# Attention scores of even and odd heads: from one half of the array's rows after the other to both by turns

## The chip, the cores and the metric

The kernel runs on one core of one Trainium2 chip. The core has a matrix engine (TensorE, PE in the profile, with its weight loads listed apart as PEld), a vector engine (VectorE, DVE), a scalar engine (ScalarE, ACT), GpSimd (POOL) and a queue engine (SyncE, SP) that issues most transfers. Matrix products land in PSUM, which is split into banks. The metric is the device time of one execution in microseconds. Three timed runs of the kernel before gave 1156.94, 1159.72 and 1166.53 us, median 1159.72.

## The reference

A retention layer without softmax feeds two mixture-of-experts layers. The part that the change touches is the first:

```python
batch, n_heads, seq, head_dim = (8, 8, 576, 64)
scores = scale * np.matmul(q, k.transpose(0, 1, 3, 2))
Dmat = np.where(rel >= 0, gamma[:, None, None] ** rel[None, :, :], 0.0)
ret = scores * Dmat[None, :, :, :]
return np.matmul(ret, v).astype(np.float32)
```

Its result, 4608 tokens of 512 numbers, goes through two layers that each pick one of eight experts for a token by the largest of eight gate logits, and multiply by that expert's two matrices (512 x 1024 and 1024 x 512). Because the choice is an argmax, the attention is computed to nearly single precision: every factor is split into a high and a low half-precision part, and a product is three products (high by high, high by low, low by high).

## The kernel before, in words

**Tiling.** `attention_and_routing` cuts the sequence of each batch into four chunks of 128 positions and a tail of 64; the tails of two batches make one more chunk, so there are 36 chunks (nine for two batches). A chunk is handled with all eight heads. Within a chunk the scores of key by query are computed, masked and multiplied by the values; what lies before the chunk comes in through a running state of 64 x 64 numbers a head. After that each token's row is scaled, gate logits are formed, a route is computed for groups of four or five chunks, and POOL scatters the rows by expert to DRAM. `experts` follows as a loop of its own, and takes most of the time.

**One chunk, by names.** `k_hi`, `k_lo`, `q_hi`, `q_lo` split the inputs (ACT and DVE). `transposes` (L330, eight products into `pt`) turns the keys, and `kT_out` copies them to `kT`. There a pair of heads lies one below the other: the even head in partitions 0 to 63, the odd head in 64 to 127, and the queries `qT` lie in the same way. `scores` (L348) multiplies them. `HALF[r]` picks the partitions, so with r = 0 a product uses rows 0 to 63 of the array and with r = 1 rows 64 to 127. For each r there are four head pairs and three products a pair, 12 products of 64 rows by 128 columns with 128 columns moving, into the PSUM tile `pa[r]`. The tags `pa0` and `pa1` have one buffer each, so a chunk's scores can't start before those of the chunk before have been read.

The two kinds are read differently. For even heads `a_full` (step `am0`, DVE, L418) masks straight from PSUM into a 32-bit tile (`a` in the profile), and `av_full` (`av0`, L402, product `po<-vs,a`) multiplies it at full precision. For odd heads `a_hi` (`ah1`, ACT, `au`) and `a_lo` (`al1`, DVE, L280, `al`) split, `mask` (`mh1`, `ml1`, POOL) masks, and `av` (`av1`, `po<-vh,ah` and `po<-vh,al`) multiplies. `qS` (`qS0`, `qS1`, product `po<-Sh,qT`) adds the state's share, `kv` (L375, L377) makes the next state in `pS`, which `Sn` (L381) scales. `out` (L429) reads `po` into `xg` once for each chunk. `lg` (L460) forms the gate logits from a row that a DMA has transposed.

**Order.** Nothing is scheduled at run time. `PLAN` gives each step five numbers, one for each position c of a chunk in its batch (the fifth is the tail); step n of chunk i is sorted at i + PLAN[n][c], and each engine gets its instructions in that order and works them off one after the other. The rows that the change touches are

```python
    "S0": (-0.000, -0.451, -0.122, 0.179, 0.057),
    "am0": (0.222, 0.032, 0.531, 0.449, 0.187),
    "S1": (0.334, 0.281, 0.287, 0.260, 0.137),
```

`S0` and `S1` are the scores of even and of odd heads: two steps, with other work between them on PE for most chunks.

Of the kernel before, what the change touches and what calls it, by code (L numbers as in the profile page):

```python
# [13 lines left out]
F32 = mybir.dt.float32  # L14
# [5 lines left out]
B, H, S, HD = 8, 8, 576, 64  # L20
D, F, E = 512, 1024, 8
N = B * S
P = 128
# [11 lines left out]
PLAN = {  # L35
    "k_hi": (-2.028, -2.770, -3.081, -2.909, -2.763),
    "vs": (-1.992, -2.348, -3.188, -1.669, -1.282),
    "k_lo": (-1.751, -2.064, -2.527, -2.579, -2.639),
    "q_hi": (-1.097, -1.702, -1.683, -2.485, -2.161),
    "pt": (-1.401, -1.677, -1.460, -1.290, -1.005),  # L40
    "v_hi": (-0.811, -1.371, -1.336, -0.862, -0.420),
    "q_lo": (-0.551, -1.252, -1.482, -1.253, -0.584),
    "v_lo": (-0.297, -1.046, -0.245, -0.372, 0.196),
    "kT": (-1.159, -0.874, -0.403, -0.701, -0.998),
    "S0": (-0.000, -0.451, -0.122, 0.179, 0.057),
    "am0": (0.222, 0.032, 0.531, 0.449, 0.187),
    "S1": (0.334, 0.281, 0.287, 0.260, 0.137),
    "kv": (0.073, 0.524, 0.372, 0.505, 1.633),
    "Sn": (0.230, 0.575, 0.613, 0.695, 6.213),
    "ah1": (0.596, 0.631, 0.385, 0.518, 0.232),  # L50
# [61 lines left out]
def attention_and_routing(tc, st, I, K):  # L112

    nc = tc.nc
# [3 lines left out]
    ps = psum("ps", 1)  # L118
# [152 lines left out]
    HALF = (slice(0, 64), slice(64, 128))  # L271
# [14 lines left out]
    class Chunk:  # L286
# [54 lines left out]
        def q_lo(self):  # L341
            lo(self.qT[:, 1], self.qn, self.qT[:, 0], QS)

        def scores(self, r):
            self.pa[r] = ps.tile([P, 512], F32, tag=f"pa{r}", name=f"pa{self.tag}_{r}")
            for hp in range(4):
                for n, (x, y) in enumerate(PASSES):
                    nc.tensor.matmul(self.pa[r][:, hp * P:(hp + 1) * P], self.kT[HALF[r], 4 * x + hp, :], self.qT[HALF[r], y, hp, :], start=(n == 0), stop=(n == 2))  # L348

        def a_hi(self, r):  # L350
            self.au[r] = three.tile([P, 512], F16, bufs=3, tag="au", name=f"au{self.tag}_{r}")
# [113 lines left out]
    for i, x in enumerate(order):  # L465
# [6 lines left out]
        "vs": Chunk.v_scale, "k_hi": Chunk.k_hi, "k_lo": Chunk.k_lo, "q_hi": Chunk.q_hi, "q_lo": Chunk.q_lo, "v_hi": Chunk.v_hi, "v_lo": Chunk.v_lo,  # L472
        "pt": Chunk.transposes, "kT": Chunk.kT_out, "kv": whole(Chunk.kv), "Sn": whole(Chunk.state),
        "Sh": whole(Chunk.state_hi), "Sl": whole(Chunk.state_lo), "out": Chunk.out, "sq": Chunk.squares,
        "rs1": Chunk.row_scale, "rs2": Chunk.row_scale2, "xh": Chunk.x_hi, "xl": Chunk.x_lo, "lg": Chunk.logits,
    }
    for n, f, r in (("S0", Chunk.scores, 0), ("S1", Chunk.scores, 1), ("am0", Chunk.a_full, 0), ("av0", Chunk.av_full, 0),
                    ("qS0", Chunk.qS, 0), ("qS1", Chunk.qS, 1), ("ah1", Chunk.a_hi, 1), ("al1", Chunk.a_lo, 1), ("av1", Chunk.av, 1)):
        parts[n] = lambda x, f=f, r=r: f(x, r)
    for n, part in (("mh1", 0), ("ml1", 1)):  # L480
# [5 lines left out]
    for i, x in enumerate(order):  # L486
        for L in "kqv":
            add(i - 5.5, x.load, L)
        for n, beats in PLAN.items():
            when = beats[x.c]  # L490
            if i >= NT - 2:
                when = {"qS0": PLAN["S1"][x.c] - 0.001, "qS1": PLAN["av1"][x.c] + 0.001}.get(n, when)
            if n in ("k_hi", "k_lo", "q_hi", "q_lo", "vs", "v_hi", "v_lo") and i < len(FIRST):
                when += FIRST[i]
            add(i + when, parts[n], x)
# [923 lines left out]
def build(nc, I, off, outs):  # L1419
    with ExitStack() as st:  # L1420
        sb = lambda n, s, dt: st.enter_context(nc.sbuf_tensor(n, s, dt))[:]
        K = {"off": off}
        K["cst"] = sb("cst", [P, max(b for _, b in off.values())], F32)
        K["ones"], K["tri"] = sb("ones", [P, P], F16), sb("tri", [P, P], F16)
        K["wg2"] = sb("wg2", [P, 4, 24], BF16)
        K["bias"] = sb("bias", [P, 16], F32)
        K["reg1"] = sb("reg1", [1, 24], I32)
        K["zero"] = sb("zero", [P, XW], F32)
        K["wb0"] = sb("wb0", [P, 2, 8192], F16)
        K["xs1"] = nc.dram_tensor("xs1", [E * R, XW], F32, kind="Internal").ap()  # L1430
        K["xs2"] = nc.dram_tensor("xs2", [E * R, XW2], F32, kind="Internal").ap()
        with tile.TileContext(nc) as tc, ExitStack() as s2:
            attention_and_routing(tc, s2, I, K)
        experts(nc, st, I, K, outs[0])
# [46 lines left out]
```

## Time and profile before

| | us |
|---|---|
| median of three timed runs | 1159.72 |
| lowest and highest | 1156.94, 1166.53 |
| the profiled execution | 1168.55 |
| span of the profiled execution, first to last instruction | 1166.8 |
| score products (L348), 864 of them, busy time | 84.5 |

The span falls into the attention and routing (to about 305 us), a change-over, and the experts from 327.5 us on. The profile's line PEclk gives the clock that TensorE was granted, as a share of full speed: 0.50 is 1.2 GHz and 1.00 is 2.4 GHz, and the trace shows only these two. In the attention the clock goes back and forth between them; in the experts it stands at 1.00 nearly throughout. Busy time of PE counts a product from its start to its end, and products overlap, so for the cost of a block of products the start of the block and the start of the next one are read from the timeline.

### The profile page before, as it was taken

What the parts mean: (1) busy time and instruction counts of PE and PEld (TensorE: products, weight loads), DVE (VectorE), ACT (ScalarE), POOL (GpSimd) and SP (SyncE); (2) the same over time, 40 slices, a digit from 0 to 9 for tenths busy, and PEclk for the clock granted to TensorE, in tenths of its full rate; (3) what the DMA queues carried; (4) which work ended last, traced back from release to release, by engine and by line L of the source; (5) the groups of instructions that cost most, each with busy time, mean ns of one, the idle gap of its engine ahead of it and who ended that gap; (6) DMA issues with size and microseconds to landing.
All of it is one profiled execution on the core that took longest, in us unless ns stands there. A gap on an engine that the chain in (4) does not pass through costs nothing. (4 is left out here: it accounts for less than half of the span.)

```text
span 1166.8 us, 27289 instructions
## 1 busy us (share of the span) xinstructions
PE 1083.7 (93%) x10037; PEld 788.2 (68%) x10037; DVE 572.4 (49%) x1624; ACT 441.6 (38%) x833; POOL 334.0 (29%) x370
## 2 busy tenths in 40 slices
PE   8999889998179999999999989999999999999996
PEld 6888778887156676666666657676766666767664
DVE  6567988996645555555555564641421211111211
ACT  5556656663324343443434433431411111111111
POOL 6456866885511211112121231211001000001000
PEclk6556768685589999999999999999999999999999
DMA  8254756675466665657466646435421121121110
GB/s 286 56 146 91 215 169 166 184 209 154 119 218 184 144 148 143 167 121 188 93 201 156 147 126 156 125 75 170 90 56 55 45 64 38 46 56 54 45 37 30
DMA packets 213056, 145.07 MB, mean 124 GB/s; under 512 B 174089, under 2 KB 174253, under 8 KB 212912
## 3 DMA queue, kind: packets, MB, share of 16 engines
q1 hardware_dynamic: 203952, 114.63, 39.9%
q0 software_dynamic: 8960, 28.62, 6.9%
q8 instruction: 79, 1.29, 0.5%
q14 instruction: 65, 0.53, 0.2%
HBM read 70.75 MB, written 33.92 MB: 90 GB/s over the span
## 5 line engine op out<-in xcount | busy, mean ns | idle before, releaser
L1060 PE MATMUL ph<-xT,wb 128*128 128x256 f16 (+2 forms) x1344 | 339.1, 263 | 22.4 <-PEq L564 22.4
L1061 PE MATMUL ph<-xT,wb 128*128 128x256 f16 (+2 forms) x1344 | 339.2, 263 | 0.0
L1062 PE MATMUL ph<-xT,wb 128*128 128x256 f16 (+2 forms) x1344 | 339.1, 263 | 0.0
L1268 DVE SCALAR_TENSOR_TENSOR hT<-ph,hT 128x512 f16<-128x512 f32 (+2 forms) x168 | 106.5, 638 | 333.7 <-DVEq L564 332.0
L1068 PE MATMUL py<-wb,hT 128*128 128x512 f16 x608 | 230.3, 379 | 1.2 <-issue 1.1
L1070 PE MATMUL py<-wb,hT 128*128 128x512 f16 x608 | 230.4, 379 | 0.0
L1069 PE MATMUL py<-wb,hT 128*128 128x512 f16 x608 | 230.4, 379 | 0.0
L1159 ACT ACTIVATE hT<-ph 128x512 f16<-128x512 f32 (+2 forms) x168 | 92.9, 553 | 227.2 <-ACTq L564 227.1
L1060 PEld LDWEIGHTS ph<-xT,wb 128*128 128x128 f16 x1344 | 131.7, 98 | 40.3 <-issue 23.1
L1061 PEld LDWEIGHTS ph<-xT,wb 128*128 128x128 f16 x1344 | 131.7, 98 | 17.1
L1062 PEld LDWEIGHTS ph<-xT,wb 128*128 128x128 f16 x1344 | 131.8, 98 | 13.1
L1386 POOL DMA_INDIRECT out_dram<-yo,idxo x37 | 35.9, 971 | 333.1 <-POOLq L564 329.7
L1375 POOL TENSOR_SCALAR idx<-v_pos 128x1 int32<-128x1 f32 x39 | 15.4, 394 | 336.3 <-POOLq L564 336.3
L1070 PEld LDWEIGHTS py<-wb,hT 128*128 128x128 f16 x608 | 59.4, 98 | 71.8
L1068 PEld LDWEIGHTS py<-wb,hT 128*128 128x128 f16 x608 | 59.3, 98 | 66.7 <-issue 1.2
L1069 PEld LDWEIGHTS py<-wb,hT 128*128 128x128 f16 x608 | 59.3, 98 | 64.9
L348 PE MATMUL pa<-qT,kT 64*128 64x128 f16 x864 | 84.5, 272 | 7.7 <-DVE al L280 6.1
L1153 ACT ACTIVATE yo<-py,v_gcol 128x512 f32<-128x512 f32 x37 | 25.4, 687 | 168.2 <-ACTq L564 168.2
L576 DVE SCALAR_TENSOR_TENSOR wb<-stg,wb 128x2048 f16<-128x2048 f32 x36 | 82.4, 2290 | 11.0 <-DVEq L564 11.0
L348 PEld LDWEIGHTS <-kT 64*128 64x128 f16 x864 | 69.4, 122 | 13.9 <-DVE al L280 6.8
L1136 ACT ACTIVATE wb<-stg 128x2048 f16<-128x2048 f32 x36 | 68.5, 1901 | 0.0
L1147 ACT ACTIVATE sq<-py 128x512 bf16<-128x512 f32 x39 | 23.3, 597 | 111.6 <-ACTq L564 111.6
(175 smaller groups left out, 1479.9 us busy)
## 6 DMA issues: line engine op xcount, KB each, us to landing
stg<-in_moe_w_dram SPq DMA_DIRECT2D x36, 1024.0 KB, 5.1
kn<-in_k_dram SPq DMA_DIRECT2D x36, 256.0 KB, 6.4
qn<-in_q_dram SPq DMA_DIRECT2D x36, 256.0 KB, 4.5
vn<-in_v_dram SPq DMA_DIRECT2D x36, 256.0 KB, 3.4
w0s<-in_moe_w_dram SPq DMA_DIRECT2D x16, 256.0 KB, 4.7
xs<-zero SPq DMA_DIRECT2D x8, 262.0 KB, 2.7
xs<-zero SPq DMA_DIRECT2D x8, 258.0 KB, 2.9
xT<-xs SPq DMA_TRANSPOSE x42
```

The lines of the kernel that those rows point to most:

```text
L348: nc.tensor.matmul(self.pa[r][:, hp * P:(hp + 1) * P], self.kT[HALF[r], 4 * x + hp, :], self.qT[HALF[r], y, hp, :], start=(n == 0), stop=( ...
L576: r = fn(*a, **kw).then_inc(self.sem, 1)
L1060: pe.matmul(o, w1(P_, 0)[:, c, fs], xT[s][:, c, cs], start=(c == 0), stop=False)
L1061: pe.matmul(o, w1(P_, 0)[:, c, fs], xT[s][:, 4 + c, cs], start=False, stop=False)
L1062: m = pe.matmul(o, w1(P_, 1)[:, c, fs], xT[s][:, c, cs], start=False, stop=(c == 3))
L1068: pe.matmul(py[b], hT[:, 0, f, bs], w2(P_, 0)[:, f, :], start=(f == 0), stop=False)
L1069: pe.matmul(py[b], hT[:, 0, f, bs], w2(P_, 1)[:, f, :], start=False, stop=False)
L1070: m = pe.matmul(py[b], hT[:, 1, f, bs], w2(P_, 0)[:, f, :], start=False, stop=(f == 7))
L1136: ac.activation(wb[P_ % 2][:, 0, 2048 * c:2048 * c + 2048], stg[:, 2048 * c:2048 * c + 2048], AF.Copy, scale=WS).then_inc(T["cv_full"])
L1159: ac.activation(hT[:, 0, 2 * g:2 * g + 2, cs], ph[g][:, :, cs], AF.Relu).then_inc(T["hh_full"])
L1268: stt(hT[:, 1, 2 * g:2 * g + 2, cs], ph[g][:, :, cs], 0.0, hT[:, 0, 2 * g:2 * g + 2, cs], op0=ALU.max, op1=ALU.subtract).then_inc(T["h_full"])
L1386: po.indirect_dma_start(out=out, out_offset=bass.IndirectOffsetOnAxis(ap=idxo[b], axis=0), in_=yo[b], in_offset=None, bounds_check=N - 1, ...
```

## The change

The steps `S0` and `S1` become one step `S`, which issues the products of even and odd heads by turns: the first of r = 0, the first of r = 1, the second of r = 0, and so on. Each kind still goes to its own bank. The step stands nearly where `S1` stood, and `am0` is moved behind it.

```diff
-    "S0": (-0.000, -0.451, -0.122, 0.179, 0.057),
-    "am0": (0.222, 0.032, 0.531, 0.449, 0.187),
-    "S1": (0.334, 0.281, 0.287, 0.260, 0.137),
+    "S": (0.222, 0.181, 0.287, 0.260, 0.097),
+    "am0": (0.334, 0.282, 0.531, 0.449, 0.187),
...
-        def scores(self, r):
-            self.pa[r] = ps.tile([P, 512], F32, tag=f"pa{r}", name=f"pa{self.tag}_{r}")
+        def scores(self):
+
+            for r in range(2):
+                self.pa[r] = ps.tile([P, 512], F32, tag=f"pa{r}", name=f"pa{self.tag}_{r}")
             for hp in range(4):
                 for n, (x, y) in enumerate(PASSES):
-                    nc.tensor.matmul(self.pa[r][:, hp * P:(hp + 1) * P], self.kT[HALF[r], 4 * x + hp, :], self.qT[HALF[r], y, hp, :], start=(n == 0), stop=(n == 2))
+                    for r in range(2):
+                        nc.tensor.matmul(self.pa[r][:, hp * P:(hp + 1) * P], self.kT[HALF[r], 4 * x + hp, :], self.qT[HALF[r], y, hp, :], start=(n == 0), stop=(n == 2))
...
-                when = {"qS0": PLAN["S1"][x.c] - 0.001, "qS1": PLAN["av1"][x.c] + 0.001}.get(n, when)
+                when = {"qS0": PLAN["S"][x.c] - 0.001, "qS1": PLAN["av1"][x.c] + 0.001}.get(n, when)
```

What that does to the order is seen on PE where chunk 0 of the second batch passes into chunk 1. A name such as `pa_0_1` is the score tile of position 0, odd heads; `kT_0` belongs to position 0. Before:

```order
L348 MATMUL pa_0_0_766<-qT_0_602,kT_0_600 128x128
...
L375 MATMUL pS_0_779<-vh_0_632,kh_0_465 64x64
...
L402 MATMUL po_3_713<-vs_3_388,a_3_674 128x64 x4
L348 LDWEIGHTS kT_0_600
L348 MATMUL pa_0_1_822<-qT_0_602,kT_0_600 128x128
...
L330 MATMUL pt_2_850<-id_69,kh_2_604 128x128
...
L348 MATMUL pa_1_0_859<-qT_1_660,kT_1_809 128x128
...
L402 MATMUL po_0_891<-vs_0_471,a_0_815 128x64 x4
...
L348 MATMUL pa_1_1_916<-qT_1_660,kT_1_809 128x128
```

And in the changed kernel, the same place:

```order
L377 MATMUL pS_0_766<-vh_0_632,kh_0_452 64x64
...
L404 MATMUL po_3_713<-vs_3_388,a_3_674 128x64 x4
L350 LDWEIGHTS kT_0_600
L350 MATMUL pa_0_0_802<-qT_0_602,kT_0_600 128x128
...
L350 MATMUL pa_0_1_803<-qT_0_602,kT_0_600 128x128
...
L329 MATMUL pt_2_850<-id_69,kh_2_604 128x128
...
L404 MATMUL po_0_878<-vs_0_458,a_0_833 128x64 x4
...
L350 MATMUL pa_1_0_895<-qT_1_660,kT_1_796 128x128
...
L350 MATMUL pa_1_1_896<-qT_1_660,kT_1_796 128x128
```

The even heads' scores of position 0 have moved behind the state products `pS_0` and the values' products `po_3`, those of position 1 behind the products `po_0`, and each block now holds both kinds. Between the block of position 0 and the products `po_0` that need its even half there remain the eight transposes and twelve products of `av`.

DVE at the same place (`al` reads odd scores, `a` even ones, `xg` reads a finished chunk). Before:

```order
L280 TENSOR_TENSOR al_0_1_889<-pa_0_1_822,au_0_1_873 128x512
L418 TENSOR_TENSOR a_1_908<-pa_1_0_859,mc 128x512
L429 TENSOR_TENSOR xg_3_910<-po_3_713,cst 128x512
L282 SCALAR_TENSOR_TENSOR kh_4_914<-kn_4_544,kh_4_914 128x512
L381 TENSOR_TENSOR Sn_1_969<-pS_1_942,cst 128x256
```

And in the changed kernel:

```order
L279 TENSOR_TENSOR al_0_1_876<-pa_0_1_803,au_0_1_860 128x512
L431 TENSOR_TENSOR xg_3_921<-po_3_713,cst 128x512
L420 TENSOR_TENSOR a_1_927<-pa_1_0_895,mc 128x512
L281 SCALAR_TENSOR_TENSOR kh_4_925<-kn_4_544,kh_4_925 128x512
L383 TENSOR_TENSOR Sn_1_969<-pS_1_942,cst 128x256
```

The masking `a_1` has moved behind `xg_3`. The orders of ACT and POOL are the same in both kernels.

## Rows read from the trace of the kernel before

**Rows 1.** The page: busy shares; the span in 40 slices of 29.2 us.
```profile
PE 1083.7 (93%) x10037; PEld 788.2 (68%) x10037; DVE 572.4 (49%) x1624; ACT 441.6 (38%) x833; POOL 334.0 (29%) x370
...
PEclk6556768685589999999999999999999999999999
```

**Rows 2.** Busy time by stretch, from:to, length, then engines, clock, DMA share, GB/s.
```profile
11.45:110.43 98.98, 98.98 (x1148) 86.63 (x1147) 61.65 (x130) 53.89 (x102) 54.19 (x59) 0.50 0.45 136
264.03:292.50 28.47, 26.39 (x331) 22.91 (x329) 17.81 (x57) 10.39 (x23) 13.36 (x15) 0.50 0.57 150
...
327.50:1166.80 839.30, 809.29 (x6258) 550.28 (x6258) 325.17 (x1011) 259.10 (x478) 124.60 (x154) 0.99 0.43 110
```

**Rows 3.** The same view: the three low-clock stretches from 130.91 to 243.55.
```profile
sum 75.09, PE 71.96 PEld 63.63 DVE 62.10 ACT 46.32 POOL 53.77; mean PE 23.99 PEld 21.21 DVE 20.70 ACT 15.44 POOL 17.92
```

**Rows 4.** The same view: the four full-clock stretches from 110.43 to 264.03.
```profile
110.43:130.91 20.48, 17.41 (x351) 15.41 (x352) 20.10 (x44) 15.02 (x31) 17.42 (x18) 1.00 0.82 208
...
sum 78.51, PE 67.38 PEld 59.62 DVE 76.66 ACT 54.35 POOL 64.13; mean PE 16.84 PEld 14.90 DVE 19.17 ACT 13.59 POOL 16.03
```

**Rows 5.** The same view, score products (L348) alone, PE and PEld.
```profile
11.45:110.43 98.98, 33.75 (x288) 27.99 (x288) 0.50 0.45 136
```

**Rows 6.** The same view, L429 alone on DVE, once for each chunk.
```profile
110.43:264.03 153.60, 14.29 (x21) 0.76 0.69 184
```

**Rows 7.** PE's timeline at the low clock: start us, us, instructions merged.
```profile
19.64 1.46 PE L348 MATMUL pa<-qT,kT 64*128 64x128 f16 x12
21.02 0.86 PE L375 MATMUL pS<-vh,kh 128*64 128x64 f16 x24
...
22.36 0.82 PE L402 MATMUL po<-Sh,qT 64*128 64x64 f16 x12
23.11 1.04 PE L330 MATMUL pt<-id,kh 128*128 128x128 f16 x8
```

**Rows 8.** PE's timeline, a chunk whose two score blocks stand side by side.
```profile
35.73 2.29 PE L348 MATMUL pa<-qT,kT 64*128 64x128 f16 x24
37.95 0.40 PE L330 MATMUL pt<-id,kh 128*128 128x128 f16 x2
```

**Rows 9.** PE's timeline, state products followed by score products.
```profile
84.83 0.28 PE L348 MATMUL pa<-qT,kT 64*128 64x128 f16 x1
84.87 0.24 PE L402 MATMUL po<-Sh,qT 64*128 64x64 f16 x1
84.90 0.31 PE L348 MATMUL pa<-qT,kT 64*128 64x128 f16 x1
```

**Rows 10.** PE's timeline at the full clock.
```profile
116.24 0.84 PE L348 MATMUL pa<-qT,kT 64*128 64x128 f16 x12
117.01 0.57 PE L375 MATMUL pS<-vh,kh 128*64 128x64 f16 x24
```

**Rows 11.** Who waited for whom, DVE, 11.45 to 110.43: us, times, longest.
```profile
DVE xg L429 <- PE po L402: 16.3, 10, 3.4
DVE Sn L381 <- PE pS L377: 8.9, 8, 1.8
DVE a L418 <- PE pa L348: 6.3, 8, 1.9
```

**Rows 12.** Score products just before the clock rose; the last stretch had no rise.
```profile
107.00:110.43 3.43, 0.00 (x0) 0.00 (x0) 0.50 0.35 128
150.40:154.50 4.10, 0.00 (x0) 0.00 (x0) 0.50 0.58 145
182.85:185.52 2.67, 0.00 (x0) 0.00 (x0) 0.50 1.02 270
240.10:243.55 3.45, 0.00 (x0) 0.00 (x0) 0.50 0.31 118
63.05:69.55 6.50, 0.00 (x0) 0.00 (x0) 0.50 0.43 107
```

**Rows 13.** PE's timeline where the clock fell, at 130.91.
```profile
130.52 1.13 PE L348 MATMUL pa<-qT,kT 64*128 64x128 f16 x12 [3.07 <-DVE al L280]
```

More of the change, by code (lines that the diff above doesn't have):

```diff
@@ L474, in attention_and_routing @@
         "Sh": whole(Chunk.state_hi), "Sl": whole(Chunk.state_lo), "out": Chunk.out, "sq": Chunk.squares,
-        "rs1": Chunk.row_scale, "rs2": Chunk.row_scale2, "xh": Chunk.x_hi, "xl": Chunk.x_lo, "lg": Chunk.logits,
+        "S": Chunk.scores, "rs1": Chunk.row_scale, "rs2": Chunk.row_scale2, "xh": Chunk.x_hi, "xl": Chunk.x_lo, "lg": Chunk.logits,
     }
-    for n, f, r in (("S0", Chunk.scores, 0), ("S1", Chunk.scores, 1), ("am0", Chunk.a_full, 0), ("av0", Chunk.av_full, 0),
+    for n, f, r in (("am0", Chunk.a_full, 0), ("av0", Chunk.av_full, 0),
                     ("qS0", Chunk.qS, 0), ("qS1", Chunk.qS, 1), ("ah1", Chunk.a_hi, 1), ("al1", Chunk.a_lo, 1), ("av1", Chunk.av, 1)):
```

## The prediction, made before the changed kernel ran

> **What bounds the kernel now.** I read four views in this order. The page first: PE is busy for 93% of the span, but its clock line is far from full in the first eleven slices and full after that [rows 1]. So the span is two programs, and the change touches only the first. The experts from 327.50 us on run at clock 0.99 [rows 2]; no instruction there changes, and I cost them at nothing.
>
> Then the busy times by stretches of equal clock. From 11.45 to 110.43 us the clock is granted at 0.50 (1.2 GHz) and PE is busy for 98.98 of 98.98 us, DVE for 61.65, ACT and POOL for some 54 [rows 2]. What DVE waits for there is PE: for the finished chunk 16.3 us, for the state 8.9, for the scores 6.3 [rows 11]. So in this stretch PE alone sets the pace. Its 288 score products [rows 5] are 12 chunks, so a chunk takes 98.98 / 12 = 8.25 us. From 110.43 to 264.03 the clock alternates. In its full-clock stretches (1.00, 2.4 GHz) DVE is busy for 76.66 of 78.51 us and PE for 67.38 [rows 4]: DVE bounds. In its low-clock stretches PE is busy for 71.96 of 75.09 us, DVE for 62.10 [rows 3]: PE bounds, with less to spare. This part has 21 chunks [rows 6], or 153.60 / 21 = 7.31 us each, and DVE alone needs (76.66 + 62.10) / 21 = 6.61.
>
> Last, PE's timeline for the price of a block. At the low clock 12 score products start at 19.64 and the next block at 21.02 [rows 7]: 1.38 us. At the full clock it is 117.01 - 116.24 = 0.77 us [rows 10].
>
> **Do both halves work at once?** The trace of before shows it by accident. Where the two score blocks stand side by side, 24 products take 37.95 - 35.73 = 2.22 us instead of 2 x 1.38 = 2.76 [rows 8]. And a score product on one half started at 84.83, ahead of a state product on the other half at 84.87, with the next score product at 84.90 [rows 9]: the two kinds run through each other. State updates, which write the two halves of the columns by turns, three and three, put 24 products into 0.86 us, where 12 products of the same 64 moving columns on one half of the rows take 0.82 [rows 7]. What is unseen is a whole block alternated by rows. I take full overlap. From the side-by-side block: 12 products fill 1.38 us, and the second half's start is offset by a fraction of a product, so 24 take about 1.44 us at the low clock and, by the same ratio, 0.80 at the full one. The other end, no overlap, is 2 x 1.38 = 2.76.
>
> The Trainium skill's page "TensorE: Matmul & The Clock Gate", section "Back-to-back issue gap", says that a stream of load and product pairs sustains 81 ns a product at 128 columns. By that, as an estimate, 24 products take 1.94 us and the change loses at the full clock, where two blocks now cost 1.54. The trace disagrees: 24 state products, each with a load of its own, take 0.57 us there [rows 10].
>
> **The change part by part**, against the profiled execution of 1168.55 us (8.83 above the median of 1159.72; I carry the saving over unchanged).
>
> *A, 11.45 to 110.43.* A chunk saves 2.76 - 1.44 = 1.32 us. Two of the twelve already have the side-by-side form and save 2.22 - 1.44 = 0.78. That is 10 x 1.32 + 2 x 0.78 = 14.8 us if the clock stays low, and a chunk then takes (98.98 - 14.8) / 12 = 7.01 us. DVE, with 61.65 / 12 = 5.14 a chunk, doesn't stop that. If the clock were full throughout, DVE's 61.65 us would be the floor and the saving 37.3: these are the two ends. Which is nearer? The four rises all came while PE was as busy as before them but after 2.7 to 4.1 us without any score product [rows 12]; the long low stretch holds such products for 33.75 us of busy time [rows 5]. One stretch of 6.50 us without them brought no rise [rows 12], so this is not the whole condition. After the change score blocks take about half the time and fill both halves of the rows, so I expect the clock to rise earlier and to be full for some of the stretch, as it is for 78.51 of 153.60 us later [rows 3, 4]. I take one third of the way from 14.8 to 37.3: **22 us**.
>
> *B, 110.43 to 264.03.* In the full-clock stretches DVE has 1.85 us left [rows 4], so nothing comes from there. In the low-clock stretches DVE has 75.09 - 62.10 = 12.99 us left [rows 3], and some 10 chunks pass (75.09 / 7.31); 10 x 1.32 = 13.2 us would be freed on PE. The ends are 0 and 13, and I take **6**: half, because DVE is close behind.
>
> *C, 264.03 to 292.50.* PE is busy for 26.39 of 28.47 us at the low clock and DVE for 17.81 [rows 2], but each chunk's chain of steps shows here, since nothing fills behind it. Two chunks at 1.32 us bound it by 2.6, and nothing is the other end; **2**. What follows (routes, scatters, change-over) moves as one piece.
>
> *Moved steps.* Only PE's and DVE's orders change; ACT, POOL and the transfers stand as before. `S0` goes later, up to where `S1` was. The even scores of position 0 are then closer to their use: between the block and `po<-vs,a` PE has eight transposes and twelve value products, 1.04 us and, priced as the twelve state products, 0.82 [rows 7], about 1.9 us at the low clock. The masking needs the last product's drain, 0.31 [rows 9], and a DVE instruction of the kind of `xg`, 14.29 / 21 = 0.68 [rows 6], about 1.0. At the full clock PE's cover shrinks by the ratio 0.77 / 1.38 to about 1.0 and is gone if DVE is late; behind the waiting product stand the state products and the scores of position 1. One DVE instruction late, 0.7 us, at eight such places is 5.6 us at most, and nothing if DVE comes in time. The first score product must now also wait until the odd bank has been read by `al` of the chunk before; where it stood alone, it waited for the even bank only. I take **2** together, the nearer end, since at the low clock there is cover.
>
> Sum: 22 + 6 + 2 - 2 = 28. Profiled: 1168.55 - 28 = 1140.6; as a median 1159.72 - 28 = **1132 us**.
>
> **The rivals.**
>
> *The clock stays as it is* (25%). Then A gives 14.8 and the rest 6: 21 us, 1139. For it: the stretch without scores that brought no rise [rows 12]. Against it: the other four. The Trainium skill's page "TensorE: Matmul & The Clock Gate", in "What's actually happening", lets the clock follow how busy PE has been; by that rule the change gives PE more idle time and no earlier rise. Here PE was busy throughout a stretch at 0.50 [rows 2], so busy time alone doesn't explain the level.
>
> *DVE takes the gain back* (12%): no rise in A, nothing in B, C or the tail, 14.8 less 2 for the waits, so about 1147. For it: DVE's 76.66 of 78.51 us [rows 4].
>
> *The halves don't run at once when alternated* (6%). Then 24 products take 2.76 us and only places move: no change, 1160. Against it [rows 8, 9].
>
> *A ring between DVE and PE* (5%), the slow side. The block waits for `al` of the chunk before, and DVE's next even masking waits for the whole block, so both engines stand still by turns. If DVE had nothing between, it would idle for the block and its last product's drain, 1.44 + 0.31 = 1.75 us a chunk, 36 x 1.74 = 63 us; less the 28 gained this is 1195. It decides from 28 / 36 = 0.8 us a chunk. For it: PE already stood 3.07 us for `al` once, and the clock fell at once [rows 13]. Against it: in the new order of DVE a finished chunk (`xg`) and other steps stand between the two.
>
> **The numbers.** The forecast has 52%; its own range is 1117 (A at its far end, 15 us more) to 1146 (A at 14.8, B at 0). A measurement of this kernel tells about 1%, some 12 us, from no change. Below 1148 lie nearly all of the forecast, most of the second case and half of the third: 80% faster. No change takes the rest of these and the halves that don't overlap: 15%. Slower, the ring: 5%. The range 1116 to 1150 leaves out the no-overlap case, the ring, and a few per cent at the low end.
>
> **What would show it.** A block of 24 score products of about 1.4 us at clock 0.50 and 0.8 at 1.00; PE no longer busy throughout the first 100 us, or the clock 1.00 in part of them; DVE's busy share there up from 62% to 75% or more; attention's end some 28 us earlier, the experts' length unchanged. I am wrong if a block takes over 2 us, if PE's waits for `al` and `a` grow by more than 0.8 us a chunk, or if the clock falls oftener than it rises earlier.

## The result, and the profile after

Four runs of the changed kernel took 1127.39 to 1131.96 us, median 1129.8; four of the kernel before took 1156.94 to 1166.53, median 1162.81. The ratio is 0.972, with a 95% interval of 0.9667 to 0.9773. The forecast was 1132 us. Ratios and their intervals here leave out a kernel's runs that lie more than 1.5% above its fastest; on one chip the kernel before ranged from 1144.09 to 1176.62 us in 19 runs, so there a ratio lies nearer to 1 than the two medians do.

The profiled execution took 1131.96 us, its span 1130.2 (before 1166.8). The page, as in [rows 1]:

```profile
PE 1025.8 (91%) x10037; PEld 736.6 (65%) x10037; DVE 579.8 (51%) x1624; ACT 439.8 (39%) x833; POOL 338.2 (30%) x370
...
PEclk8858787865899999999999999999999999999999
```

PE is busy for 57.9 us less, DVE for 7.4 us more with the same 1624 instructions (more on that below), and the clock line starts with 8 8 5 8 where 6 5 5 6 stood.

To compare stage by stage I cut both spans at the same work instead of at the same clock: from 12 us to the start of the 11th finished chunk (`xg`), to the 32nd, to the 36th, to the first expert product, and to the end. The columns are those of [rows 2]. The kernel before, cut in this way:

```profile
12.00:111.28 99.28, 99.28 (x1158) 87.07 (x1157) 61.95 (x132) 54.65 (x103) 54.60 (x59) 0.50 0.45 136
111.28:265.93 154.65, 140.39 (x2250) 123.96 (x2249) 139.81 (x315) 100.50 (x198) 118.95 (x122) 0.75 0.68 182
265.93:292.58 26.65, 24.57 (x300) 21.47 (x299) 15.91 (x56) 9.72 (x21) 11.46 (x13) 0.50 0.61 160
...
327.55:1166.82 839.27, 809.29 (x6258) 550.26 (x6258) 325.17 (x1011) 259.10 (x478) 124.60 (x154) 0.99 0.43 110
```

And the changed kernel:

```profile
12.00:86.01 74.01, 67.71 (x1159) 59.82 (x1154) 65.71 (x132) 53.59 (x103) 59.17 (x59) 0.70 0.62 181
86.01:231.93 145.92, 117.71 (x2253) 103.13 (x2253) 142.74 (x316) 99.54 (x198) 118.27 (x122) 0.80 0.74 193
231.93:253.47 21.54, 19.42 (x291) 17.64 (x291) 16.56 (x57) 9.72 (x21) 11.66 (x13) 0.58 0.68 184
...
288.56:1130.15 841.59, 810.39 (x6258) 550.47 (x6258) 325.20 (x1011) 259.30 (x478) 125.01 (x154) 0.99 0.43 109
```

I call these stages A, B, C and the experts. They save 99.28 - 74.01 = 25.3, 154.65 - 145.92 = 8.7, 26.65 - 21.54 = 5.1 and -2.3 us; the change-over before the experts is equal to 0.1 us. That makes 36.7 us of span. Read the DVE column beside the length: in A, PE was busy for every microsecond before and DVE for 62% of them; now DVE is busy for 89%, and in B for 98%. In B the bound has passed from PE to DVE. In A it still changes with the clock. The same view for the four stretches of A at 0.50 (12.57 to 19.39, 33.05 to 36.46, 39.87 to 46.70 and 56.94 to 84.25), and for the three at 1.00 between them:

```profile
sum 44.37, PE 42.82 PEld 38.04 DVE 38.27 ACT 28.32 POOL 32.98; mean PE 10.71 PEld 9.51 DVE 9.57 ACT 7.08 POOL 8.25
...
sum 27.31, PE 22.56 PEld 19.64 DVE 25.10 ACT 22.95 POOL 23.86; mean PE 7.52 PEld 6.55 DVE 8.37 ACT 7.65 POOL 7.95
```

At the low clock PE is still the busier engine, 42.82 of 44.37 us; at the full one it is DVE, 25.10 of 27.31.

PE's timeline, as in [rows 7, 10], first at the low clock, then at the full one:

```profile
16.26 1.46 PE L350 MATMUL pa<-qT,kT 64*128 64x128 f16 x24
17.66 0.86 PE L377 MATMUL pS<-vh,kh 128*64 128x64 f16 x24
...
21.41 0.84 PE L350 MATMUL pa<-qT,kT 64*128 64x128 f16 x24
22.18 0.57 PE L377 MATMUL pS<-vh,kh 128*64 128x64 f16 x24
```

From start to start, 24 products by turns take 17.66 - 16.26 = 1.40 us at 1.2 GHz and 22.18 - 21.41 = 0.77 at 2.4 GHz: what 12 took before. The overlap is complete.

Who waited for whom in A, B and C, DVE and PE (us, times, longest). The kernel before, 12 to 290 us:

```profile
DVE xg L429 <- PE po L402: 20.7, 15, 3.4
DVE Sn L381 <- PE pS L377: 13.0, 13, 2.0
DVE a L418 <- PE pa L348: 11.6, 13, 1.9
...
PE pa L348 <- DVE al L280: 6.1, 2, 3.1
```

And the changed kernel, 12 to 253 us:

```profile
PE pa L350 <- DVE al L279: 17.7, 10, 3.7
...
DVE a L420 <- PE pa L350: 10.8, 16, 1.9
...
DVE xg L431 <- PE po L404: 1.5, 2, 1.2
...
DVE Sn L383 <- PE pS L377: 0.4, 1, 0.4
```

DVE's waits for finished chunks and for the state are nearly gone. PE in turn stands 17.7 us before score blocks until DVE's `al` has read the odd bank, 6.1 before. Where DVE is the slower engine, that wait costs little by itself; this is argued from the busy shares, and no run shows it.

### The profile page after: what moved, and what is told of

Read it like the earlier page. It is cut to its first block, busy times and chain, and to the rows that moved or that the text cites. A ratio compares the mean times of both kernels' runs of the same rounds, so it can differ in the third digit from the quotient of the medians.

```text
span 1130.2 us, 27289 instructions
## 1 busy us (share of the span) xinstructions
PE 1025.8 (91%) x10037; PEld 736.6 (65%) x10037; DVE 579.8 (51%) x1624; ACT 439.8 (39%) x833; POOL 338.2 (30%) x370
## 5 line engine op out<-in xcount | busy, mean ns | idle before, releaser
L1062 PE MATMUL ph<-xT,wb 128*128 128x256 f16 (+2 forms) x1344 | 338.7, 263 | 22.5 <-PEq L566 22.5
L1381 POOL DMA_INDIRECT xs<-x2row,idx x39 | 50.3, 1290 | 37.5 <-POOLq L566 37.5
L350 PE MATMUL pa<-qT,kT 64*128 64x128 f16 x864 | 43.9, 260 | 18.1 <-DVE al L279 17.7
```

The source lines that it names most:

```text
L1062: pe.matmul(o, w1(P_, 0)[:, c, fs], xT[s][:, c, cs], start=(c == 0), stop=False)
L1381: po.indirect_dma_start(out=xs2, out_offset=bass.IndirectOffsetOnAxis(ap=idx[b], axis=0), in_=x, in_offset=None, bounds_check=E * R - 1, o ...
```

## The experiments

Of A, B and C the lengths, the granted clock and DVE's busy share are read from the same view and cuts for each kernel, one profiled execution each (of "before, 8 and 8 apart" it was the fastest of the ten):

| kernel | A us, clock, DVE | B us, clock, DVE | C us, clock | median us (runs) |
|---|---|---|---|---|
| before | 99.3, 0.50, 0.62 | 154.7, 0.75, 0.90 | 26.7, 0.50 | 1162.81 (4) |
| before again | 94.9, 0.56, 0.64 | 162.7, 0.69, 0.88 | 26.5, 0.50 | 1172.76 (1) |
| changed | 74.0, 0.70, 0.89 | 145.9, 0.80, 0.98 | 21.5, 0.58 | 1129.80 (4) |
| changed again | 74.9, 0.78, 0.87 | 146.4, 0.74, 0.95 | 22.0, 0.66 | 1134.62 (6) |
| 12 and 12 by kind | 79.0, 0.72, 0.82 | 156.1, 0.69, 0.91 | 24.9, 0.50 | 1150.40 (4) |
| three and three | 74.3, 0.77, 0.89 | 145.8, 0.78, 0.97 | 19.5, 0.76 | 1132.23 (2) |
| six and six | 73.8, 0.75, 0.89 | 146.0, 0.81, 0.98 | 19.1, 0.75 | 1129.03 (1) |
| 8 and 8 by kind | 75.0, 0.68, 0.87 | 147.3, 0.72, 0.97 | 22.2, 0.50 | 1131.74 (4) |
| before, 8 and 8 apart | 72.6, 0.70, 0.90 | 147.3, 0.79, 0.97 | 22.5, 0.50 | 1135.46 (10) |
| 48 by turns | 74.7, 0.89, 0.86 | 148.2, 0.89, 0.92 | 22.6, 0.88 | 1139.33 (4) |
| 24 and 24 by kind | 87.9, 0.79, 0.73 | 165.6, 0.81, 0.80 | 26.8, 0.72 | 1182.27 (2) |
| a DVE step on ACT | 69.6, 0.73, 0.84 | 133.8, 0.83, 0.95 | 19.6, 0.74 | 1119.18 (4) |
| `iv` once for a group | 73.5, 0.78, 0.91 | 146.6, 0.76, 0.95 | 21.8, 0.80 | 1136.56 (6) |
| block earlier | 78.3, 0.76, 0.82 | 156.2, 0.73, 0.89 | 22.3, 0.50 | 1144.69 (10) |

Theory: the block is cheaper because the two halves of the rows work at once; PE falls behind DVE, and DVE's time is the new floor; the clock rises earlier because blocks are shorter and fill both halves. The rivals: the place and the merging into one step do it; only the clock does it; a ring of waits takes part of it back.

### The two kernels once more

> The kernel before once more, for a second profile. By kind in one block gave 20 us in the first stretch, with the clock at 0.72 there in place of 0.50, though only four pairs of products run together. Either the 0.50 throughout is what the kernel before always does there (then one block in place of two is what brings the clock up), or it was one execution's luck: then the first eleven chunks end at 85 to 100 us here, not at 111, and the clock rises once or twice before that.

> The changed kernel once more, as the base for the two others on this chip. About 1130 us, ratio to the kernel before near 0.972; the stretch from 12 us to the eleventh finished chunk near 74 us at a clock of about 0.70.

The kernel before took 1172.76 us, and its clock rose for 10 us near the end of A, where it had not in the first trace. Its A and B are 4.4 us shorter and 8.0 longer than in the first profile. So single stages of a kernel at PE's bound move by several us with the clock, and I read nothing into less. The changed kernel on another chip took 1134.62 us at the median (1127.70 to 1141.25), beside 1158.12 of the kernel before there: 23.5 us less, ratio 0.9811 (0.9759 to 0.9863). Its A, B and C agree with the first within 1 us, though the clock was 0.78, 0.74 and 0.66 in place of 0.70, 0.80 and 0.58; the experts took 2.2 us more.

### How fine the turns must be

```diff
-            for hp in range(4):
-                for n, (x, y) in enumerate(PASSES):
-                    for r in range(2):
+            for r in range(2):
+                for hp in range(4):
+                    for n, (x, y) in enumerate(PASSES):
```

> The changed kernel with its new places, but with the twelve even products issued first and the twelve odd ones after them. My theory (the gain comes from issuing by turns): a block of 24 takes 2.2 us at the low clock and 1.3 at the full one, as the side-by-side block did in the kernel before; the clock in the first 100 us stays mostly at 0.50; some 8 us faster than before, about 1152. The rival (the gain comes from the new places of the steps): as fast as the changed kernel, about 1130.

PE's timeline of this kernel, low clock:

```profile
12.64 2.29 PE L350 MATMUL pa<-qT,kT 64*128 64x128 f16 x24
14.86 1.04 PE L329 MATMUL pt<-id,kh 128*128 128x128 f16 x8
```

The block takes 14.86 - 12.64 = 2.22 us, as the side-by-side block of before [rows 8]: only the products around the seam overlap. The kernel took 1150.40 us, ratio 0.9883 (0.9794 to 0.9972). On that chip this is 13.1 us below the median of the kernel before, so merging and moving alone, with that seam, bring about 0.4 of the gain. It lies in A, which fell to 79.0 us at a clock of 0.72, where I had expected mostly 0.50; B gained nothing that shows.

With the loop over r between the pairs and the passes (three and three), and with two pairs of one kind at a time (six and six):

```diff
-                for n, (x, y) in enumerate(PASSES):
-                    for r in range(2):
+                for r in range(2):
+                    for n, (x, y) in enumerate(PASSES):
```

and

```diff
+            for h2 in range(2):
+                for r in range(2):
+                    for hp in (2 * h2, 2 * h2 + 1):
+                        for n, (x, y) in enumerate(PASSES):
...
```

> Three even products of a head pair, then three odd ones, by turns. If PE reaches a few products ahead on the other half (four pairs ran together in the side-by-side block), a block takes 1.4 us at the low clock and 0.8 at the full one, and the time is 1130. If the turn has to change with each product, a block takes 1.8 us or more at the low clock and the time is 1140.

> Six and six by turns. With a reach of four products: each of the three changes of half brings four pairs together, so all twelve, or nearly, and a block takes 1.4 to 1.6 us at the low clock. If the reach ends at the change of half only, 2.0 us.

A block of six and six, low clock:

```profile
33.24 1.65 PE L351 MATMUL pa<-qT,kT 64*128 64x128 f16 x24
34.83 1.03 PE L329 MATMUL pt<-id,kh 128*128 128x128 f16 x8
```

34.83 - 33.24 = 1.59 us instead of 1.40 (at the full clock 0.90 instead of 0.77); by threes a block takes 1.40, as by ones. Both kernels took as long as the changed one (1132.23 us, ratio 0.9712, 0.9622 to 0.9803; and 1129.03 us in a single run). Single turns aren't needed: one half after the other would take 2.76 us, so around each change of half several products run through each other, as those of two steps did in [rows 9], and turns of up to six keep both halves at work for most of the block.

### A shorter block without filled halves

Here the third of the three passes is left out: once in the changed kernel, in one block by kind:

```diff
+            for r in range(2):
                 for hp in range(4):
-                    for n, (x, y) in enumerate(PASSES):
-                        for r in range(2):
+                    for n, (x, y) in enumerate(PASSES[:2]):
...
```

> As by kind, but the third of the three products of each head pair (low keys by high queries) is left out, 8 and 8 products, so that a block takes about as long as the changed kernel's (1.36 us at the low clock, by the 2.22 us of 24 less 8 products of 0.107) while the halves of the rows are mostly filled one at a time. If the shorter block alone makes the gain, 1130 as the changed kernel. If filling both halves also brings the clock up earlier, the clock stays at 0.50 for most of the first 85 us, chunks take about 7.0 us there, and the time is 1137 to 1142.

and once in the kernel before, with its two steps in their old places:

```diff
-                for n, (x, y) in enumerate(PASSES):
+                for n, (x, y) in enumerate(PASSES[:2]):
...
```

> The kernel before with its two separate score blocks, each with 8 products in place of 12 (the product of low keys by high queries is left out). A chunk has 0.86 us less on PE at the low clock, less than by turns saves (1.36), and no block is moved or merged. If less time on PE is what counts, the first stretch shortens by 10 us or more, the clock rises earlier, and the time is 1140 to 1150. If the two steps must stand together for the clock to rise, the first stretch stays at 0.50 and saves 10 us alone, 1150 to 1155.

The first took 1131.74 us, ratio 0.9701 (0.9631 to 0.9772), as much gain as the change. The second took 1135.46 us at the median, beside 1166.68 of the kernel before on that chip; ratio 0.9878 (0.9804 to 0.9953), its profiled execution 1126.89. Both lie below the 1140 to 1150 that I gave. The stages of the second:

```profile
12.00:84.64 72.64, 70.74 (x1062) 61.15 (x1061) 65.09 (x131) 53.21 (x103) 58.51 (x59) 0.70 0.62 187
84.64:231.96 147.32, 123.39 (x2079) 106.85 (x2079) 143.08 (x315) 99.69 (x198) 120.80 (x122) 0.79 0.72 191
```

A clock of 0.70 and DVE busy for 65.09 of 72.64 us, with two separate blocks, each on one half, in the old order. So neither the filled halves nor the merging nor the place is needed for earlier rises: here they came with less PE time at this point alone. Against the forecast's reason for the clock, this is a miss.

### The same PE time with filled halves, and without

The block issued twice (the second set writes the same scores over the first), by turns:

```diff
-            for hp in range(4):
-                for n, (x, y) in enumerate(PASSES):
-                    for r in range(2):
...
+            for again in range(2):
+                for hp in range(4):
+                    for n, (x, y) in enumerate(PASSES):
+                        for r in range(2):
...
```

> The changed kernel with the whole block of score products issued twice, still by turns (48 products instead of 24; the second set writes the same scores over the first). From the changed kernel's pace of 50.1 ns a product at the low clock and 27.3 at the full one, 48 products take about 2.6 and 1.4 us: nearly what the two separate blocks took before (2.76 and 1.54), but as one block, in the new place and with both halves of the rows filled. Theory (PE's time alone lifts the clock, not the form of the block): the stretch from 12 us to the eleventh finished chunk is back at 92 to 99 us with the clock at 0.50 to 0.56 as in the two traces of the kernel before, and the run takes 1155 to 1168 us. Rival (one block that fills both halves keeps the clock up whatever it takes): that stretch stays below 82 us at a clock of 0.68 or more, and the run takes 1130 to 1145.

and with 24 even products followed by 24 odd ones:

```diff
-            for hp in range(4):
-                for n, (x, y) in enumerate(PASSES):
-                    for r in range(2):
...
+            for r in range(2):
+                for again in range(2):
+                    for hp in range(4):
+                        for n, (x, y) in enumerate(PASSES):
...
```

> The same 48 score products as in the kernel that issues the block twice by turns, in one block in the same place, but 24 even ones and then 24 odd ones. From the block of 24 by kind (12 take 1.38 us at the low clock, and 0.54 us are saved where the kinds meet) 48 take 2 x 2.76 - 0.54 = 5.0 us at the low clock and about 2.8 at the full one, against 2.67 and 1.4 by turns. Theory (products that leave half of the rows empty hold the clock down, and filled ones lift it): the stretch from 12 us to the eleventh finished chunk runs at a clock of 0.50 to 0.65 and takes 100 to 120 us, and the run takes 1210 to 1290 us. Rival (more products in one block lift the clock, whichever half they use): the clock there is 0.80 or more as it was by turns (0.89), that stretch takes at most 90 us, and the run takes 1145 to 1180 us.

The timeline of the first, at the low and the full clock:

```profile
12.74 2.74 PE L351 MATMUL pa<-qT,kT 64*128 64x128 f16 x48
15.41 1.03 PE L329 MATMUL pt<-id,kh 128*128 128x128 f16 x8
...
17.94 1.51 PE L351 MATMUL pa<-qT,kT 64*128 64x128 f16 x48
19.38 0.57 PE L378 MATMUL pS<-vh,kh 128*64 128x64 f16 x24
```

and its stages:

```profile
12.00:86.66 74.66, 66.56 (x1499) 59.90 (x1498) 64.09 (x132) 54.08 (x104) 59.13 (x59) 0.89 0.66 181
86.66:234.89 148.23, 122.21 (x2700) 109.89 (x2695) 136.52 (x316) 98.95 (x196) 118.82 (x122) 0.89 0.76 190
```

48 products by turns take 2.67 us at the low clock, nearly the 2.76 of the two old blocks [rows 7]. The clock did not fall back to 0.50 as my theory then had it: at 0.89 it was the highest of all. PE's time alone doesn't set the clock; the rival was right here. The run took 1139.33 us, ratio 0.9867 (0.9804 to 0.9931). So A fell to 74.66 us with score products that cost nearly as much at either clock as in the kernel before (2.67 and 1.44 us against 2.76 and 1.54): a higher clock can do it without a shorter block. How much of A's 25.3 us in the changed kernel comes from shorter blocks and how much from earlier rises, no run separates.

Was it the filled halves? The stages of the 48 by kind:

```profile
12.00:99.87 87.87, 85.59 (x1435) 79.15 (x1430) 63.77 (x132) 53.87 (x103) 57.03 (x59) 0.79 0.58 154
99.87:265.51 165.64, 157.89 (x2754) 145.98 (x2754) 132.40 (x315) 99.11 (x197) 114.91 (x122) 0.81 0.68 170
```

0.79 and 0.81, with PE busy for 97% and 95%: above the kernel before, below 0.89. My expectation of 0.50 to 0.65 was wrong as well; two runs took 1167.28 us (the profiled one) and 1197.25. Filled halves went with a higher clock than the same products by kind in five of six pairs of stages (24: 0.70 to 0.72, 0.80 to 0.69, 0.58 to 0.50; 48: 0.89 to 0.79, 0.89 to 0.81, 0.88 to 0.72), but fewer products and more products of one kind raised it too. **What sets the clock is left open.** What a still higher one is worth can be read: the changed kernel (twice), three and three, and six and six ran A at 0.70 to 0.78 and took 73.8 to 74.9 us for it, and B at 0.74 to 0.81 for 145.8 to 146.4, the shortest A and B not at the highest clock. With DVE so near its own floor, a higher clock gave nothing more over this range.

### Does DVE bound now?

The low part of `xr` (a DVE instruction of two tensors, 36 times) gives way to a second copy on ACT, so the kernel leaves out the low part:

```diff
-            nc.vector.scalar_tensor_tensor(self.xr[:, 512:1024], self.xg, self.of("sc"), self.xr[:, 0:512], op0=ALU.mult, op1=ALU.subtract)
+            nc.scalar.activation(self.xr[:, 512:1024], self.xg, AF.Identity, scale=self.of("sc"))
```

> The changed kernel with the low part of each scaled row made on ACT as a second copy of the high part (so the row's value is doubled; the routes stay), which takes 36 DVE instructions of 0.74 to 1.0 us away and gives ACT 36 of 0.71. If DVE bounds the attention now (98% busy in the middle), it ends 15 to 25 us earlier and the time is 1105 to 1115. If PE or the transfers bound it, 1125 to 1135.

```profile
12.00:81.58 69.58, 64.25 (x1117) 56.37 (x1113) 58.25 (x123) 57.13 (x110) 56.55 (x58) 0.73 0.69 194
81.58:215.33 133.75, 112.22 (x2222) 98.58 (x2220) 126.93 (x294) 110.02 (x219) 111.27 (x121) 0.83 0.79 211
```

It took 1119.18 us (1116.38 to 1121.34), below every run of the changed kernel; ratio to the kernel before 0.9737 (0.9616 to 0.9857). Against the changed kernel's trace A loses 4.4 us and B 12.2, and DVE's busy time in B falls by 142.74 - 126.93 = 15.8. So B loses three quarters of what DVE loses: DVE is its floor. The attention ended 18.5 us earlier (234.94 against 253.47), inside the 15 to 25 that I gave, but the time missed the 1105 to 1115: the change-over and the experts took 5.2 us more (37.36 + 844.49 against 35.09 + 841.59), which I can't explain; the experts' part, 2.9, lies within their spread over all kernels here, 835.8 to 845.4.

A small version of the same idea that leaves nothing out: `iv`, 0.14 us, once for a group of chunks.

```diff
+        v.tensor_scalar(iv[:, g].bitcast(I32), gr.eb[:, g], 8388608.0, 59.0 * 8388608.0, op0=ALU.mult, op1=ALU.add)
...
-            v.tensor_scalar(self.of("iv").bitcast(I32), self.of("eb"), 8388608.0, 59.0 * 8388608.0, op0=ALU.mult, op1=ALU.add)
```

> The changed kernel with one small DVE instruction (iv, 0.14 us) computed once for a group of chunks in route instead of once for each chunk: 27 fewer DVE instructions. If DVE bounds chunks 12 to 32 of the changed kernel (busy 0.98 there), up to 27 x 0.14 = 3.8 us go, and the run takes about 1126 to 1128 beside 1130 of the changed kernel on the same chip. Rival (the place at the end of a chunk is covered by a wait): no difference.

1136.56 us beside 1134.62 of the changed kernel on the same chip, ratios 0.9839 (0.9791 to 0.9888) and 0.9811 (0.9759 to 0.9863): no difference. A and B are 73.5 and 146.6 us against 74.9 and 146.4. 3.8 us of DVE are less than these intervals can tell, or lay where DVE had slack; no kernel here that computes everything beats the changed one measurably.

### Does the place matter?

The block goes 0.16 to 0.29 of a chunk earlier, and `am0` back to its old place (a third edit keeps `qS0` of the last two chunks where it was):

```diff
-    "S": (0.222, 0.181, 0.287, 0.260, 0.097),
-    "am0": (0.334, 0.282, 0.531, 0.449, 0.187),
+    "S": (0.060, -0.100, 0.000, 0.050, -0.100),
+    "am0": (0.222, 0.032, 0.531, 0.449, 0.187),
...
```

> The changed kernel with its score block 0.12 to 0.29 of a chunk earlier in the order, and the masking of the even heads where it stood before. If the order of the block matters little because DVE bounds, 1127 to 1133. If the waits between DVE and PE decide, the block now stands closer behind the step that frees its bank, waits grow and the time is 1136 or more.

It took 1144.69 us, ratio 0.9943 (0.9895 to 0.9991). B, and who waited from 12 to 253 us:

```profile
90.33:246.57 156.24, 125.98 (x2201) 110.42 (x2202) 139.67 (x315) 99.07 (x198) 119.91 (x122) 0.73 0.68 180
```

```profile
PE pa L350 <- DVE al L279: 34.5, 20, 3.6
...
DVE xg L431 <- PE po L404: 19.1, 13, 3.5
DVE a L420 <- PE pa L350: 8.6, 13, 1.6
```

In B neither PE (81%) nor DVE (89%) is busy throughout. Over the attention PE stands for `al` 34.5 us instead of 17.7, what is queued behind the block comes late, and DVE then waits 19.1 us for finished chunks instead of 1.5. This is a ring between DVE and PE like the prediction's slow rival, but it closes through the finished chunk and not through the even masking, whose wait is 8.6 us against 10.8 in the changed kernel. The block and `am0` moved together, so the run doesn't tell which of the two brings it on.

## Why the prediction was right, step by step

**The block.** Forecast 1.44 and 0.80 us with full overlap; measured 1.40 and 0.77. The 81 ns a product of the Trainium skill's page "TensorE: Matmul & The Clock Gate" ("Back-to-back issue gap") are not seen here: 0.77 us for 24 is 32 ns. The prediction set the 24 state products against that figure, but those move 64 columns each; the like case in [rows 10] is the 12 score products, 0.77 / 12 = 64 ns each on one half.

**A, 22 us.** It saved 25.3, between the ends 14.8 and 37.3. By DVE's column: DVE idled 99.28 - 61.95 = 37.3 us before and 74.01 - 65.71 = 8.3 after, which gives 29.0, and its own work grew by 3.8. Against the second profile of the kernel before it saved 20 to 21 us. That PE no longer bounds A throughout is shown; at the low clock it still does for the most part, as the rows above have it. The third of the way between the ends came from no row, so that 22 lies near 25.3 is in part luck. The *reason* given for the clock failed in part. "Fill both halves" is not needed (8 and 8 apart, 0.70), "half the time" is not needed either (48 by turns, 0.89). That it would rise earlier rested on [rows 12], where rises came after spells without score products (the second of these ended 0.3 us before the rise, with score products started at 154.53), and it did; but the two kernels with twice the score products have a higher clock than the kernel before, so the products themselves don't hold it down, and the cause stays open.

**B, 6 us.** It saved 8.7. DVE's idle time fell from 14.8 to 3.2 us, 11.7 in all, and its work grew by 2.9. DVE being "close behind" was the right reason, and it gave 6 for 8.7. The size is not firm: against the second profile of the kernel before, B saved 16 to 17 us, and DVE's work in it fell (143.04 to 142.74 or 138.36).

**C, 2 us.** Mis-sized: 5.1, beyond the bound of 2.6. That bound took the clock as 0.50 there; in this stage it was 0.58, and 0.75 and 0.76 in two other runs, with C at 19.1 and 19.5 us. The clock is not all of it, since three kernels with 0.50 throughout C (8 and 8 in both forms, and the block earlier) took 22.2 to 22.5 us for it. The cuts hold somewhat different PE products in each trace (300 before, 291 after), and what the rest is stays open.

**Moved steps, 2 us lost.** Not to be seen by itself: DVE's wait for even scores is 10.8 us in the attention, against 11.6 before. What worse places cost is seen in the kernel with the block earlier and `am0` moved back: its A, B and C are 4.3, 10.3 and 0.7 us longer than the changed kernel's.

**The experts, nothing.** They took 2.3 us more. Their instructions are the same in all kernels here and took 835.8 to 845.4 us, with one dip of the clock or several, so this is spread and no effect that I could trace.

**The rivals.** The clock did not stay; the halves do run at once; DVE did take gain back, as the bound of B, not as the whole story; the ring did not decide. Of the signs of being wrong none came: PE's waits for `al` and `a` grew from 7.5 to 18.1 us, some 0.3 us a chunk.

The sum was 28 us, and the profiled pair gave 1168.55 - 1131.96 = 36.6. The medians gave 33.0 against the four runs of before, 29.9 against the three that were known then, and 23.5 on the other chip. The profile of before was slower than its four timed runs; part of the 36.6 is that. So the sum lies among what was measured, while its terms A, B and C all fell short of this pair; that 1132 came within 3 us of 1129.80 is in part luck. Two slips in the working change nothing: the ring's 36 x 1.74 stands for 36 x 1.75, and the range's upper end, with A at 14.8 and B at 0, comes to 1145 and not 1146.

## What to carry to other kernels

When two streams of products each use one half of the array's rows and write different banks, as here, issue them by turns in small lots (up to six cost no time that shows) and price the pair as one. Before making an engine cheaper, subtract the next engine's busy time from the length of the stage: that is the most that the change can give (37.3 us in A and 14.8 in B), and no higher clock brought more here. Then check that the merged block doesn't wait for the engine that its followers feed, since its place, with that of the masking, made some 10 to 15 us here (1144.69 against 1134.62 and 1129.80, on different chips).

## Not expected

Some of DVE's instructions grew longer, though the change doesn't touch them. Those on the same tiles, all 36 of each in the first 330 us (count, busy us, mean ns, idle before), in the kernel before:

```profile
L451 DVE SCALAR_TENSOR_TENSOR xr<-xg,sc,xr 128x512 f16<-128x512 f32 x36 | 36.0, 1000 | 0.1
L282 DVE SCALAR_TENSOR_TENSOR kh<-kn,kh 128x512 f16<-128x512 f32 x36 | 33.8, 939 | 3.9 <-ACT kh L275 3.9
...
L280 DVE TENSOR_TENSOR al<-pa,au 128x512 f16<-128x512 f32 x36 | 24.5, 679 | 3.1 <-ACT au L275 3.1
```

and in the changed one:

```profile
L281 DVE SCALAR_TENSOR_TENSOR kh<-kn,kh 128x512 f16<-128x512 f32 x36 | 40.9, 1136 | 3.6 <-ACT kh L274 3.6
L453 DVE SCALAR_TENSOR_TENSOR xr<-xg,sc,xr 128x512 f16<-128x512 f32 x36 | 39.0, 1084 | 0.1
...
L279 DVE TENSOR_TENSOR al<-pa,au 128x512 f16<-128x512 f32 x36 | 24.3, 676 | 0.0
```

`al`, which reads PSUM, costs the same. `kh` and `xr`, which read two tensors from SBUF, grew by 7.1 and 3.0 us, so that their means stand far above the mean of `al`. The second pair of profiles has the same for these two (30.9 to 37.6 and 35.8 to 39.9 us), but not for DVE as a whole: its busy time over the span grew by 0.9 us there (574.5 to 575.4) and not by 7.4, so that is not shown to belong to the change. A short and a long `kh` in the changed kernel's timeline:

```profile
55.40 0.68 DVE L281 SCALAR_TENSOR_TENSOR kh<-kn,kh 128x512 f16<-128x512 f32 x1
...
99.06 3.65 DVE L281 SCALAR_TENSOR_TENSOR kh<-kn,kh 128x512 f16<-128x512 f32 x1
```

and what POOL did at these places:

```profile
55.41 1.17 POOL L369 TENSOR_SCALAR_AFFINE_SELECT ah<-au 128x512 f16<-128x512 f16 x1
...
98.80 0.65 POOL L369 TENSOR_SCALAR_AFFINE_SELECT ah<-au 128x512 f16<-128x512 f16 x1
99.40 1.05 POOL L317 TENSOR_TENSOR vs<-vn,cst 128x512 f32<-128x512 f32 x1
100.40 0.64 POOL L369 TENSOR_SCALAR_AFFINE_SELECT al<-al 128x512 f16<-128x512 f16 x1
101.00 1.15 POOL L324 TENSOR_TENSOR vh<-vs,vh 128x512 f16<-128x512 f32 x1
```

At 55.40 `kh` starts first and takes 0.68 us, and POOL's `ah` behind it 1.17 instead of 0.65. At 99.06 POOL is first: `kh` lasts 3.65 us while POOL works through four instructions without a gap, and ends 0.56 us after the last of them (99.06 + 3.65 against 101.00 + 1.15). That is what the Trainium skill's page "SBUF — State Buffer", section "Who interferes with whom", states: a DVE instruction with two SBUF inputs and a GpSimd instruction that reads SBUF exclude each other, and the second blocks. The trace agrees, also in that `al` is spared. No run here separated the two engines' work: that this is the cause of all the growth, and how much of B it costs, is not shown.
